# A new order of all 2328 operations of a gated attention/FFT kernel on one core

## The chip, the core and the metric

The kernel runs on one core of one Trainium2 chip. The metric is the device time of one execution in microseconds (us), and the time of a kernel is the median of several executions. One profiled execution is recorded beside them. In it every instruction has a start, a duration and an engine: TensorE (PE, with its weight loads PEld), VectorE (DVE), ScalarE (ACT), GpSimd (POOL) and SyncE (SP, which here only issues DMAs).

## What is computed

The input x has 2048 rows of 640 bf16 values. Two branches work on it, and a gate of its own for each row mixes them:

```python
g = _sigmoid((x * gate_w).sum(-1, keepdims=True))
a = _A_ref(x, A_wq, A_wk, A_wv, A_wo, A_beta)
b = _B_ref(x, B_w_r, B_w_i)
return g * a + (1 - g) * b
```

Branch A is attention with 32 heads of 20 dimensions over four segments of 512 rows, with a memory that is carried from segment to segment:

```python
for s in range(N):
    qs, ks, vs = ...
    p = _softmax(jnp.einsum('bhqd,bhkd->bhqk', qs, ks) * scale + mask, axis=-1)
    a_dot = jnp.einsum('bhqk,bhkd->bhqd', p, vs)
    pq = phi(qs)
    a_mem = einsum('bhld,bhde->bhle', pq, M) / (einsum('bhld,bhd->bhl', pq, z)[..., None] + 1e-06)
    outs.append(g * a_mem + (1.0 - g) * a_dot)      # this g is sigmoid(beta), one for each head
    pk = phi(ks)
    M = M + einsum('bhld,bhle->bhde', pk, vs)
    z = z + einsum('bhld->bhd', pk)
return o @ wo                                       # o: the four outs, 2048 x 640
```

Branch B is a filter in frequency space: a two-dimensional real FFT of x, a product with the complex weights `w_r + i w_i`, and the inverse FFT.

## The kernel before

**A recorded program.** `Kern.record()` records the kernel as 2328 operations. An operation is a closure that writes one or more instructions, with what it reads and writes, a cost for each engine that may carry it, and a latency. `mms` (L495) records a group of matmuls; its instructions show as L514 in the profile, those of the output projection, which are split into four narrow matmuls, as L512. `copy_alts` (L519) gives a copy out of PSUM to ScalarE or VectorE; `one`, `either` and `small` record elementwise work; `dma` (L543) records a DMA, a transposing one (L546) or a plain one (L548). Nearly all DMAs are issued by SP; the two operations in `EARLY`, the first halves of the loads of wq and wk, may also be issued by ScalarE.

**An order written out.** `ORDER` (L578 to L677) is a list of 2328 numbers. Entry v stands for operation v//2, carried by its alternative v%2 (0 is the first engine of its list, 1 the second). `Sched.schedule` hands the operations to the queues of the engines in this order. Each engine carries out its queue strictly in that order, and an instruction that waits for a semaphore holds up all that stand behind it on the same engine. With the costs of the operations, `schedule` replays the list on a modelled clock; what comes out of the model is not the order but two allocations: which of eight PSUM banks (four for the logits, `qk`, four for all else, `gen`) an operation gets, and which of 56 DMA semaphores. A bank or a semaphore that was used before brings a wait for its former users:

```python
for v in order:
    o = ops[v // 2]
    o.eng = list(o.alts)[v % 2]
    queue[o.eng].append(o)
...
_, b.pool, b.bank = place(b, level)
...
o.dyn.extend(users.get(q, ()))
```

**The stages.** In the first 26 us SP loads x transposed (`xT`, segment 0 in three pieces), the weights and eight tiles of plain x (`xsb`, `ld_x`), which VectorE and GpSimd fold for the FFT. PE first runs ten matmuls on a zeroed tile, then the projections of segment 0 (`projd` in the code; `psum<-xT,wq` and `psum<-xT,wk`) as `xT` and the weights arrive. From then on attention and FFT are interleaved. The main work of attention for segment s and head group is: the logits (`qk`, matmuls that read `qkp`, the padded q and k that come back by `pad` DMAs from a scratch in HBM, `qk_scr`), the exponential on ScalarE (`ex`, L1263), the mask on GpSimd (L1284) and the products with v (`pv`).

**The end of the kernel.** The memory part of segments 1 to 3 goes over HBM: `st_part` and `ld_den` bring the denominators together, `den_gate` makes their reciprocals, `st_r` stores them (`r_scr<-rc`), `ld_r` loads them in another layout (`r<-r_scr`), and `normal` multiplies by them. The unnormalised output is stored (`st_u`) and loaded again (`ld_u`) for the rows, the memory output is written to `o_scr` (`st_o`) and comes back transposed by `oT` (`mT<-o_scr`, L546). The rows are finished in tiles of 128, by `finish_tile(s,a)` (L1506) for segment s and tile a of its four; operations are named with this pair below. `oT(s,a)` brings the tile's memory output, `addmem(s,a)` (L1534, `oU<-oU,mT`) adds it to the attention output, `Fb(s,a)` (`psum<-G,fbg`) makes the FFT branch's rows with the gate in them, `oproj(s,a)` adds the product with wo in the same PSUM bank, `final(s,a)` (`ot<-psum`) copies the bank out, and `st_out(s,a)` stores the tile (`out_dram<-ot`). Segment 3 takes its o by transposes on PE (`oT3`) and wo in another layout, which `ld_wo2` loads (800 KB).

**Entries that are spoken of below.** 24 and 25 are `ld_wka`, the first half of wk, on SP and on ScalarE; 26, 28 and 30 are the three `xT` loads of segment 0; 36 is `ld_beta`; 46 is the `ld_x` of the first fold; 3392 is a `pad` of segment 3; 4028 is `ld_r(0)`; 4418 and 4452 are `oT(1,3)` and `oT(2,3)`; 4288 is `st_out(2,1)`; 4510 is `ld_wo2`.

Of the kernel before, what the change touches and what calls it, by code (L numbers as in the profile page):

```python
# [461 lines left out]
class Kern:  # L462
# [10 lines left out]
    def b(self, *key):  # L473
        v = self.bufs.get(key)
        if v is None:
            v = self.bufs[key] = Buf(str(key))
        return v
# [20 lines left out]
    def mms(self, items, r, w, prio, name="", extra=0.0, mode=0):  # L498
# [17 lines left out]
        op = self.Sc.op({"pe": (f, cost, 141.0)}, r=r, w=w, prio=prio, name=name, mode=mode)  # L516
# [25 lines left out]
    def dma(self, dst, src, nbytes, r, w, prio, tr=False, name="", after=(), queue="sp"):  # L542
        def f(e):  # L543
            d_, s_ = dst(), src()
            if tr:
                return e.dma_start_transpose(d_, s_)  # L546
            with self.nc.allow_non_contiguous_dma(reason="small strided loads"):
                return e.dma_start(d_, s_)  # L548
        cost, work, width = self.QUEUE[name] if name in self.QUEUE else self.QUEUE[name, nbytes]
        queues = ("sp", "act") if name in self.EARLY else (queue,)  # L550
        return self.Sc.op({e: (f, cost, 0.0) for e in queues}, r=r, w=w, prio=prio, nbytes=nbytes, name=name, after=after,
                          dma=True, xfer=work, hold=tr and nbytes > 500000, width=width)
# [27 lines left out]
        46, 0, 90, 26, 74, 23, 2, 4, 36, 24, 6, 8, 28, 10, 12, 72, 14, 16, 30, 18, 20, 178, 64, 34, 202, 66, 68, 44, 42, 70, 93, 214, 52, 190, 48, 94,  # L580
        204, 97, 216, 180, 192, 218, 104, 98, 182, 76, 206, 101, 194, 38, 208, 220, 196, 103, 198, 222, 201, 184, 224, 186, 210, 188, 296, 50, 212,
        256, 298, 362, 78, 300, 536, 32, 80, 274, 538, 258, 83, 302, 260, 262, 276, 130, 278, 264, 84, 54, 280, 106, 266, 282, 1904, 86, 304, 364,
        284, 88, 366, 108, 380, 306, 576, 132, 826, 268, 290, 828, 814, 110, 368, 578, 831, 816, 113, 382, 384, 386, 819, 370, 540, 388, 832, 270,
        834, 410, 412, 272, 836, 414, 416, 391, 418, 552, 372, 490, 420, 288, 492, 494, 114, 496, 498, 554, 118, 820, 822, 134, 336, 500, 240, 137,
        338, 242, 340, 120, 348, 58, 824, 342, 116, 350, 308, 122, 312, 544, 142, 226, 932, 546, 124, 344, 292, 244, 56, 228, 144, 246, 286, 248, 347,
        139, 352, 230, 294, 232, 126, 250, 354, 146, 234, 374, 1906, 149, 237, 1908, 356, 254, 1910, 359, 2094, 151, 238, 1912, 844, 1914, 252, 2124,
        140, 2126, 1916, 2128, 128, 2130, 360, 166, 2096, 40, 846, 2098, 154, 2132, 848, 2100, 2134, 1924, 326, 1926, 314, 2102, 168, 392, 1928, 2104,
        1930, 156, 892, 310, 1932, 152, 838, 1944, 1934, 170, 334, 1946, 158, 894, 840, 324, 316, 1948, 842, 808, 897, 161, 328, 810, 1950, 1952, 394,
        320, 813, 880, 886, 163, 882, 322, 1954, 888, 560, 332, 502, 884, 504, 396, 506, 330, 172, 508, 890, 448, 376, 510, 1936, 398, 450, 436, 512,
        438, 378, 402, 452, 514, 562, 440, 174, 442, 2162, 400, 1962, 2164, 176, 444, 2166, 516, 556, 454, 456, 2168, 446, 165, 2170, 458, 464, 460,  # L590
        466, 406, 1918, 468, 462, 470, 570, 472, 408, 2172, 910, 912, 542, 474, 898, 900, 318, 914, 602, 903, 2150, 548, 604, 2152, 2154, 2156, 2158,
        1920, 2178, 572, 404, 2160, 1966, 2180, 1958, 2182, 1922, 1968, 574, 904, 60, 2184, 2174, 2186, 906, 594, 2188, 1956, 564, 908, 1970, 2176,
        580, 934, 874, 596, 876, 1972, 879, 476, 566, 1974, 62, 478, 480, 550, 1977, 868, 870, 930, 422, 568, 482, 424, 873, 484, 426, 928, 916, 558,
        486, 428, 430, 488, 918, 2136, 432, 598, 2138, 920, 2140, 434, 2142, 856, 582, 858, 1960, 2144, 922, 519, 861, 924, 606, 584, 2146, 936, 1938,
        520, 2148, 926, 588, 523, 1020, 525, 608, 586, 652, 591, 2596, 802, 654, 862, 850, 804, 864, 852, 1940, 2216, 867, 2204, 2206, 2218, 2208,
        2220, 1942, 2210, 2222, 1980, 854, 2224, 2212, 656, 634, 2226, 2214, 1978, 778, 658, 2006, 2228, 636, 780, 2230, 2008, 1982, 2190, 2010, 782,
        2012, 526, 946, 2014, 786, 784, 2192, 948, 1964, 938, 940, 942, 2194, 788, 950, 2196, 945, 2198, 952, 600, 660, 2017, 2200, 790, 662, 2202,
        792, 2018, 976, 978, 1984, 794, 2020, 958, 798, 796, 1986, 960, 980, 954, 2233, 800, 1988, 982, 610, 956, 664, 2038, 612, 1990, 528, 2236,
        2234, 1992, 965, 530, 984, 986, 2040, 1995, 534, 2076, 988, 2078, 962, 2042, 1996, 2000, 1998, 2044, 991, 614, 618, 1016, 2080, 2024, 620,
        2002, 996, 1014, 2082, 2238, 638, 998, 2084, 972, 2004, 2022, 2046, 622, 668, 974, 992, 624, 2086, 2049, 2056, 626, 1018, 994, 1070, 1072,  # L600
        2058, 1074, 666, 2060, 1022, 1076, 642, 1002, 2050, 806, 1104, 1024, 1026, 670, 645, 1001, 2062, 532, 1028, 2270, 2064, 1031, 628, 2036, 2636,
        2252, 2240, 1106, 2272, 630, 2638, 2274, 2254, 640, 2066, 2276, 2106, 676, 616, 2640, 2256, 678, 592, 2258, 1010, 1004, 2243, 2026, 966, 968,
        2052, 2070, 2028, 1013, 632, 692, 971, 1006, 694, 680, 2244, 2642, 1009, 2644, 686, 1032, 2068, 1034, 682, 2246, 646, 1100, 2054, 2090, 1036,
        2030, 2088, 684, 2288, 649, 710, 2034, 2646, 672, 2290, 1039, 2566, 712, 674, 2292, 2598, 2294, 2600, 2306, 2072, 2602, 2110, 2604, 2308,
        2606, 2074, 2568, 2310, 700, 2092, 2108, 2312, 714, 2608, 726, 2112, 2786, 703, 716, 728, 2114, 1044, 2788, 2570, 688, 1062, 1064, 1046, 2790,
        696, 1066, 2792, 2794, 2650, 1069, 690, 1040, 2796, 650, 2574, 734, 1042, 1110, 698, 1078, 736, 1108, 1082, 730, 1080, 1112, 1114, 1118, 1102,
        1120, 732, 1122, 1116, 750, 1084, 1124, 2260, 2032, 738, 752, 2278, 1049, 2578, 2262, 2280, 2264, 2580, 2282, 704, 2266, 1051, 2284, 2268,
        2296, 2582, 744, 706, 1148, 1150, 2298, 718, 2586, 2648, 754, 2300, 1058, 720, 2302, 3288, 1152, 1089, 2616, 1061, 2618, 1126, 1155, 740,
        1130, 1052, 746, 1132, 1054, 2620, 2572, 1056, 2332, 1086, 1204, 1128, 748, 1206, 2334, 1208, 2622, 2624, 2250, 756, 1096, 1211, 1090, 1135,
        1192, 1092, 2627, 762, 2118, 1095, 2576, 2610, 2390, 1194, 1137, 1098, 1196, 765, 1198, 2392, 1200, 2314, 2120, 2698, 1203, 722, 2700, 2628,  # L610
        1138, 2316, 2702, 2318, 742, 1156, 2122, 1158, 2320, 1160, 1140, 724, 708, 1163, 2704, 2630, 2324, 2612, 2116, 1142, 1168, 2654, 2614, 2706,
        770, 2326, 1170, 1164, 758, 1166, 2842, 2844, 2846, 2848, 761, 2850, 2658, 2652, 2328, 2364, 2852, 766, 2676, 2330, 2366, 2709, 2678, 1280,
        2660, 2584, 2680, 2662, 2712, 2590, 1175, 2870, 2664, 1278, 2592, 2666, 2632, 2682, 2656, 2668, 2348, 1190, 2684, 2634, 2350, 2854, 2336,
        2710, 2856, 2858, 2860, 2862, 2672, 2286, 2896, 2687, 2898, 2864, 2358, 2340, 2866, 2872, 1274, 2352, 2868, 2342, 2874, 2876, 2360, 2882,
        2816, 768, 2884, 2818, 2362, 2878, 2820, 2688, 2886, 2880, 2888, 2822, 2890, 1188, 2692, 2824, 2690, 2900, 2344, 2826, 2902, 2904, 2670, 2382,
        2368, 2828, 2892, 2384, 2830, 2894, 2832, 2346, 2748, 2834, 2906, 2750, 1242, 2370, 1244, 1246, 2752, 2674, 2836, 2376, 2694, 1248, 2716,
        2838, 2696, 2448, 2714, 772, 2338, 2754, 2354, 2450, 2730, 2732, 2356, 2840, 2734, 2736, 2756, 1173, 2738, 2372, 2741, 2758, 2386, 2422, 2588,
        2378, 2375, 1144, 2760, 2394, 1176, 2742, 1147, 2768, 1186, 2770, 2424, 2718, 2772, 2322, 2774, 2802, 2776, 2744, 1178, 2764, 3290, 2779,
        2594, 1234, 3292, 1236, 774, 1238, 2798, 2762, 2746, 2406, 2782, 3328, 1276, 1241, 2408, 3294, 3296, 2766, 3298, 2720, 3330, 2780, 3301, 1182,
# [361 lines left out]
    def gate(self, s, t_end):  # L981

        self.Sc.group += 1
        b = self.b
        prio = t_end - 1.0
# [17 lines left out]
        bank = Bank(1, "gen")  # L1003
        items = []
# [602 lines left out]
```

## Time and profile before

| | us |
| --- | --- |
| median of three runs | 243.88 (243.15 to 245.06) |
| span of the profiled execution | 245.4 |
| PE busy | 228.8 (93%), 4347 matmul instructions |
| PEld busy (beside PE) | 140.8 (57%) |
| ScalarE busy | 199.9 (81%) |
| VectorE busy | 195.6 (80%) |
| GpSimd busy | 166.4 (68%) |

The profiled execution is 1.5 us longer than the median, and 0.3 us longer than the slowest of the three runs. Times of the profile are read against its own span.

PE is the engine that is busy almost throughout; it stands still for 245.4 - 228.8 = 16.6 us in all. Busy time of matmuls is modelled at their ends, so a busy PE need not be PE at its peak. The DMA engines moved 42.2 MB, 172 GB/s on average. The costliest group is the exponential (138.7 us of ScalarE), the mask is 122.1 us of GpSimd, and neither of them fills its engine.

### The profile page before, as it was taken

How to read it: one execution, taken by the hardware profiler on the slowest of the kernel's cores; microseconds unless marked ns; L12 is line 12 of the kernel's file. 1: busy time of each engine (PE TensorE's matmuls, PEld its weight loads, DVE VectorE, ACT ScalarE, POOL GpSimd, SP SyncE). 2: the span in 40 equal slices, each digit the busy share in tenths (PEclk: the TensorE clock that was granted, in tenths of full speed). 3: DMA queues.
4: the chain of work that ended last, by engine and by line, in shares of the span. 5: the costliest groups of instructions: out<-in, count | busy, mean ns of one | idle time of the engine just before them, and what ended most of it. 6: DMA issues, size and time to landing. Idle time of an engine off the chain costs nothing.

```text
span 245.4 us, 10243 instructions
## 1 busy us (share of the span) xinstructions
PE 228.8 (93%) x4347; PEld 140.8 (57%) x4361; DVE 195.6 (80%) x481; ACT 199.9 (81%) x241; POOL 166.4 (68%) x297
## 2 busy tenths in 40 slices
PE   7899999999999999999899999899999997699994
PEld 2574567765455665545556555465454565366794
DVE  0479998889999987989999898989889867435563
ACT  2289698988999999999899889999999976388740
POOL 8513268557969846768947998859898694359730
PEclk9999999999999999999999999999999999589999
DMA  7999959975799875575698661375758997812123
GB/s 168 278 365 208 239 160 178 318 140 164 210 200 174 168 226 143 125 199 135 202 233 234 185 186 53 99 210 146 222 151 194 230 140 96 127 36 85 57 84 108
DMA packets 58928, 42.17 MB, mean 172 GB/s; under 512 B 30020, under 2 KB 55172, under 8 KB 58884
## 3 DMA queue, kind: packets, MB, share of 16 engines
q1 hardware_dynamic: 57844, 40.96, 69.2%
q8 instruction: 34, 0.56, 1.0%
q10 hardware_dynamic: 1040, 0.57, 0.8%
q14 instruction: 10, 0.08, 0.1%
HBM read 23.32 MB, written 12.30 MB: 145 GB/s over the span
## 4 chain that ended last, share of the span: by engine, by line
PE 54%; DVE 18%; ACT 12%; DMA 10%; issue 3%; SPq 1%; DVEq 0%
PE psum L514 48%; ACT ex L1263 9%; PE psum L512 6%; DMA pkn<-phk 4%; DMA r_scr<-rc 3%; DMA xT<-in_A_x_dram 2%; DVE xsb L906 2%; DVE Pt L1439 2%; DVE xf L901 1%; DVE phk L1085 1%; ACT et L1072 1%; DVE oU L1526 1%; DVE G L1485 1%; DVE ub L525 1%; DVE va L1115 1%
## 5 line engine op out<-in xcount | busy, mean ns | idle before, releaser
L1263 ACT ACTIVATE ex<-psum 128x2048 bf16<-128x2048 f32 (+4 forms) x92 | 138.7, 1507 | 16.3 <-PE psum L514 14.3
L1284 POOL TENSOR_SCALAR_AFFINE_SELECT ex<-ex 128x256 bf16<-128x256 bf16 (+2 forms) x224 | 122.1, 567 | 42.0 <-ACT ex L1263 38.4
L514 PE MATMUL psum<-qkp 20*64 20x64 bf16 (+5 forms) x1280 | 32.7, 271 | 4.8 <-issue 2.3
L514 PE MATMUL psum<-xT,wk 128*128 128x256 bf16 (+1 forms) x280 | 34.0, 273 | 0.9 <-DMA wk<-in_A_wk_dram 0.6
L514 PE MATMUL psum<-wv,xT 128*32 128x321 bf16 (+3 forms) x400 | 30.0, 301 | 0.6 <-DVE va L1115 0.3
L514 PE MATMUL psum<-xT,wq 128*128 128x512 bf16 (+1 forms) x121 | 27.0, 380 | 1.3 <-DMA xT<-in_A_x_dram 0.7
L1439 DVE TENSOR_TENSOR Pt<-psum,Wt 128x642 bf16<-128x642 f32 x32 | 25.5, 820 | 2.3 <-PE psum L514 1.9
L514 PEld LDWEIGHTS psum<-qkp 20*64 20x64 bf16 x1280 | 13.4, 103 | 19.5 <-ACT ex L1263 13.2
L514 PEld LDWEIGHTS psum<-xT,wk 128*128 128x128 bf16 (+1 forms) x280 | 19.9, 97 | 7.0 <-DMA wk<-in_A_wk_dram 1.1
L512 PE MATMUL psum<-wo,oU 128*32 128x320 bf16 x480 | 23.4, 313 | 0.5 <-DVE oU L1534 0.5
L906 POOL TENSOR_TENSOR xsb<-xf 128x320 bf16<-128x320 bf16 (+2 forms) x12 | 9.2, 763 | 17.1 <-DVE xsb L906 13.2
L525 DVE CAST ot<-psum 128x320 bf16<-128x320 f32 x21 | 10.1, 491 | 12.9 <-PE psum L512 10.5
L514 PEld LDWEIGHTS psum<-wv,xT 128*32 128x32 bf16 (+1 forms) x400 | 14.3, 96 | 8.3 <-issue 2.4
L514 PE MATMUL psum<-big,Ac 128*128 128x160 bf16 (+2 forms) x96 | 18.1, 258 | 0.7 <-DVE Pt L1439 0.3
L1115 DVE TENSOR_TENSOR va<-psum,ebx 128x320 bf16<-128x320 f32 x32 | 15.2, 483 | 4.2 <-ACT gate L1113 2.1
L514 PE MATMUL psum<-big,Cp 128*128 128x321 bf16 (+1 forms) x96 | 18.0, 302 | 0.2 <-DVE G L1485 0.2
L514 PE MATMUL psum<-ex,va 128*32 128x64 bf16 (+3 forms) x576 | 17.4, 256 | 0.7 <-DVE dn L1152 0.3
L1485 DVE TENSOR_TENSOR G<-eo,psum 128x320 bf16<-128x320 f32 x32 | 14.7, 482 | 3.9 <-PE psum L514 2.8
L512 PEld LDWEIGHTS psum<-wo,oU 128*32 128x32 bf16 x480 | 12.4, 100 | 8.8 <-issue 4.2
L514 PE MATMUL psum<-tt,Yt 128*128 128x256 bf16 (+1 forms) x96 | 16.5, 275 | 0.3
L514 PEld LDWEIGHTS psum<-ex,va 128*32 128x32 bf16 x576 | 11.1, 96 | 9.7 <-POOL ex L1284 3.4
L1072 ACT ACTIVATE et<-qu 128x512 bf16<-128x512 bf16 x25 | 15.6, 630 | 0.2
(99 smaller groups left out, 391.9 us busy)
## 6 DMA issues: line engine op xcount, KB each, us to landing
qkp<-qk_scr SPq DMA_DIRECT2D x28, 160.0 KB
tt<-tab_tt SPq DMA_DIRECT2D x8, 512.0 KB, 4.3
qk_scr<-qu SPq DMA_DIRECT2D x12, 256.0 KB, 3.1
u_scr<-ub SPq DMA_DIRECT2D x12, 256.0 KB, 3.9
xsb<-in_A_x_dram SPq DMA_DIRECT2D x8, 320.0 KB, 6.8
oU<-u_scr SPq DMA_DIRECT2D x15, 128.0 KB, 2.9
out_dram<-ot SPq DMA_DIRECT2D x12, 160.0 KB
Wt<-in_B_w_r_dram SPq DMA_DIRECT2D x16, 80.2 KB, 2.6
```

What stands on the lines that cost most here:

```text
L512: h = e.matmul(dst, wt, r_, start=st, stop=sp_, **{**kw, "tile_position": (0, q), "skip_group_check": True})
L514: h = e.matmul(o_, l_, r_, start=st, stop=sp_, **kw)
L525: alts["dve"] = (lambda e: e.tensor_copy(dst(), src()), 67 + 1.04 * n, 68.0)
L901: self.either(lambda e, r=r, op=op: e.tensor_tensor(xf.ap(r * 642, [321, 2], [1, 320]), xs.ap(o, [D, 2], [1, 320]), xs.ap(o + 320, [D, 2], ...
L906: self.either(lambda e, dst=dst, src=src, d0=d0, n=n, op=op: e.tensor_tensor(xs.ap(o + dst, [D, 2], [1, n]), xf.ap(src + d0, [321, 2], [1, ...
L1072: self.one("act", lambda e: e.activation(et.ap(0, [1, L]), qsl(), ACT.Exp), L, [qb], [b("et", pi_)], late, name="phi_exp")
L1085: fmin = lambda e: e.tensor_tensor(dst(), dst(), et.ap(0, [1, L]), ALU.min)
L1115: self.one("dve", lambda e: e.tensor_tensor(va.ap(i * H * VW + h0 * VW, [VW, nh], [1, DH]), self.ps(bank, 0, [DH, nh], [1, DH]), self.ebx. ...
L1263: self.one("act", lambda e, d=d, q=q: e.activation(self.ex.ap(*d), self.ps(bank, *q), ACT.Exp, scale=SC), n, [bank], [self.exb(s, 2 * pr + ...
L1284: self.one("pool", lambda e: e.affine_select(self.ex.ap(e0 + d0, [1280, 4], [1, n], np_=np_), self.ex.ap(e0 + s0, [1280, 4], [1, n], np_=np_),
L1439: self.one("dve", lambda e, ri=ri, Pt=Pt, Wt=Wt, wo_=wo_, bank=bank: e.tensor_tensor(Pt.ap(ri * 322, [644, 2], [1, KD]), self.ps(bank, 0, ...
L1485: self.one("dve", lambda e, q=q, n2=n2, bank=bank, eo=eo: e.tensor_tensor(self.G.ap(n2 * D + 639 * q, [1 - 2 * q, 320]), eo.ap(q, [1, 320] ...
```

## The change

Every entry of `ORDER` is written anew. The multiset of operations is the same; 131 of the 2328 change their engine (folds, copies out of PSUM, parts of `final`, gate arithmetic, and `ld_wka` from SP to ScalarE). SP goes from 232 to 231 operations, ScalarE from 249 to 246, VectorE from 481 to 485, GpSimd and PE keep their numbers. The median operation moves by three places in its engine's queue. No operation computes anything else, and none is added or left out.

Four edits beside it change costs that only the replay reads: the logits' matmuls cost 22 ns more and have a latency of 216 ns instead of 141, every DMA costs 60 ns more on its queue (110 for `st_qk`, `st_u` and `ld_u`), the first exponential of `phi` has a fixed part of 94 ns instead of 65, and the transposing matmul of the gate is taken to have the array pattern 2 instead of 0. They write no instruction differently; with the new order they change which bank and which DMA semaphore an operation gets.

```diff
@@ -513,7 +513,7 @@
-        op = self.Sc.op({"pe": (f, cost, 141.0)}, r=r, w=w, prio=prio, name=name, mode=mode)
+        op = self.Sc.op({"pe": (f, cost + 22.0 * (name == "qk"), 216.0 if name == "qk" else 141.0)}, r=r, w=w, prio=prio, name=name, mode=mode)
...
@@ -547,6 +547,7 @@
...
+        cost += 110.0 if name in ("st_qk", "st_u", "ld_u") else 60.0
...
@@ -577,103 +578,103 @@
...
-        46, 0, 90, 26, 74, 23, 2, 4, 36, 24, 6, 8, 28, 10, 12, 72, 14, 16, 30, 18, 20, 178, 64, 34, 202, 66, 68, 44, 42, 70, 93, 214, 52, 190, 48, 94,
...
-        3094, 3536, 1550, 3142, 3080, 1552, 1520, 1555, 1488, 1522, 3286, 1556, 1525, 3096, 1558, 3118, 1584, 3082, 1490, 1560, 3434, 3084, 3392,
...
-        3612, 4030, 1620, 1644, 3170, 1654, 1623, 1646, 4028, 3654, 1656, 1648, 3160, 3184, 4042, 3584, 3656, 1658, 1650, 3162, 3670, 3250, 3658,
...
-        1768, 3676, 4510, 1770, 1866, 1772, 4216, 4026, 4050, 3596, 4064, 4052, 4054, 4218, 3466, 3680, 1774, 3752, 1832, 4158, 3682, 1834, 3700,
...
-        4358, 4360, 4362, 3864, 4186, 4258, 4364, 4366, 4368, 4189, 3866, 4418, 3920, 4370, 1884, 3858, 4490, 3922, 4276, 4322, 4260, 4372, 4262,
-        3868, 4374, 4452, 4376, 4378, 4380, 4264, 4278, 4382, 4280, 4492, 4266, 3924, 4385, 3834, 4282, 3934, 3836, 4268, 4324, 4270, 4326, 3833,
-        4162, 4273, 4328, 4284, 4330, 4164, 4287, 4166, 3870, 4168, 4332, 4170, 4288, 4334, 3816, 3842, 3838, 4336, 4402, 3844, 4404, 3872, 4406,
...
+        0, 23, 26, 74, 2, 25, 4, 28, 6, 8, 10, 12, 72, 14, 30, 16, 18, 20, 46, 190, 34, 104, 90, 202, 76, 44, 36, 52, 48, 204, 206, 178, 192, 214,
+        194, 216, 180, 218, 38, 208, 196, 182, 210, 198, 213, 184, 200, 220, 186, 92, 222, 188, 94, 224, 536, 96, 98, 42, 380, 538, 256, 101, 32,
...
+        3416, 1524, 3572, 3172, 3436, 3574, 3442, 3152, 3562, 3576, 3174, 1612, 3444, 3154, 1615, 3446, 3622, 3578, 4028, 1606, 3581, 1608, 3449,
+        3583, 1574, 3196, 3430, 1610, 3624, 1577, 3156, 3606, 3176, 3392, 3626, 3158, 1652, 3628, 1654, 1634, 1636, 2562, 1638, 3178, 3608, 3614,
...
+        4287, 4270, 3924, 3834, 4272, 4493, 4324, 3868, 4326, 3836, 4288, 4328, 4162, 3870, 4380, 4164, 4330, 4418, 4382, 4166, 3934, 4332, 4385,
+        4338, 4340, 4334, 3926, 4402, 4168, 4337, 3842, 4452, 3816, 4170, 3874, 4342, 3844, 4172, 4344, 3838, 4404, 4175, 4388, 4346, 4390, 4392,
+        4190, 4290, 4406, 3846, 3848, 4394, 4348, 4396, 4510, 4398, 4408, 3840, 4292, 4350, 3878, 4352, 4304, 4420, 4306, 3880, 4294, 3876, 4401,
...
@@ -1004,7 +1005,7 @@
...
-        self.mms(items, [b("hi", s), b("lo", s), b("fcat"), bank], [], prio + 4.0, name="gateT")
+        self.mms(items, [b("hi", s), b("lo", s), b("fcat"), bank], [], prio + 4.0, name="gateT", mode=2)
...
@@ -1070,7 +1071,7 @@
...
-                     late, name="phi_exp")
+                     late, fix=94, name="phi_exp")
...
```

In the new list the start has 25 (`ld_wka` on ScalarE) and all three `xT` loads ahead of 46 (`ld_x`) and 36 (`ld_beta`); 3392 stands behind 4028; 4418 and 4452 stand directly behind 4288 on SP, while before they stood directly ahead of it; and 4510, which before stood ahead of the store and reload of the reciprocals of segment 2, is the second of SP's operations behind 4452.

## The prediction

> **What bounds the kernel now.** I read the shares of the chain that ended last first, then the slices of the span, then the two ends of the kernel operation by operation, because that is where PE stands still.
>
> ```profile
> PE   7899999999999999999899999899999997699994
> PEclk9999999999999999999999999999999999589999
> ...
> PE 54%; DVE 18%; ACT 12%; DMA 10%; issue 3%; SPq 1%; DVEq 0%
> ```
>
> Each digit of the first two lines is a fortieth of the span, 6.1 us. PE is full but for the first slices, the last, and slices 34 and 35, where its granted clock falls to 0.5 as well. PE idles 16.6 us in all; of these 3.0 lie before 8 us, 3.7 between 200 and 211.4, and 3.1 behind the last matmul. What is left, 6.8 us, is spread over many short gaps. So a new order of the same operations has three places to win or lose in: the start, the stretch from 204 us on, and the fit of the long middle, where PE is never free for long.
>
> The start, as SP's queue of DMA issues and PE's timeline show it (start, duration, operation, and in brackets the idle time before it and who ended it):
>
> ```profile
> 0.79 0.40 SPq L548 DMA_DIRECT2D xsb<-in_A_x_dram  x1
> 1.25 1.22 SPq L546 DMA_TRANSPOSE xT<-in_A_x_dram  x1
> 2.52 0.57 SPq L548 DMA_DIRECT2D beta<-in_A_beta_dram  x1
> 3.14 0.42 SPq L548 DMA_DIRECT2D wk<-in_A_wk_dram  x1
> 3.61 2.95 SPq L546 DMA_TRANSPOSE xT<-in_A_x_dram  x2
> ```
>
> ```profile
> 7.81 0.40 PE L514 MATMUL psum<-xT,wq 128*32 128x512 bf16 x4 [0.42 <-DMA xT<-in_A_x_dram]
> ```
>
> PE waits .33, .57 and .42 us at its first three projections, and the last piece of xT, issued by 6.56 us, releases it at 7.81.
>
> The end: PE's timeline, the stretches around its stall (us, busy time and count of PE, PEld, DVE, ACT, POOL, granted clock, DMA share, GB/s), the DMA answers for 204.1 to 208.7 us, and the transposes that run there.
>
> ```profile
> 208.75 0.32 PE L514 MATMUL psum<-qkp 20*64 20x64 bf16 x23
> 211.41 0.21 PE L514 MATMUL psum<-qkp 20*64 20x64 bf16 x1 [2.35 <-issue]
> ```
>
> ```profile
> 209.40:211.40 2.00, 0.00 (x0) 0.00 (x0) 0.55 (x2) 0.00 (x0) 0.41 (x1) 0.50 0.90 103
> 211.40:216.20 4.80, 4.79 (x69) 2.43 (x72) 1.39 (x4) 2.74 (x4) 1.50 (x3) 0.50 0.75 117
> 216.20:223.00 6.80, 6.80 (x205) 4.45 (x197) 2.60 (x6) 5.56 (x6) 5.34 (x10) 1.00 0.20 49
> ```
>
> ```profile
> q1 hardware_dynamic: 804, 0.46, 87.3%
> ...
> mT<-o_scr SPq DMA_TRANSPOSE x2, 7.2
> ```
>
> The stall of 2.35 us falls between matmul 23 and 24 of one operation; the 24th waits for no semaphore, hence "issue". I read it as PE short of instructions. The profile has a queue of 34 instruction packets of 16 KB, that is one for every 256 instructions of PE by the counts of this trace. Mostly one starts 0.3 to 1.5 us after PE crosses into a new block; here PE crossed at 204.12, no packet ran in the window above, where two mT transposes were landing, and it ran at 208.76, 4.64 us late. PE then ran again 1.5 us after it had come. The clock stayed at 0.5 until 216.2: 4.8 us of busy PE at half rate are about 2.4 us lost. Stall and clock together cost 4.75 us.
>
> **The change part by part.** All prices are against the profiled 245.4 us. The median of the runs is 1.52 below it, and I subtract that at the end.
>
> *Start.* Ahead of the second xT load SP loses the issues of ld_x (.40), beta (.57) and the first half of wk (.42): 1.40 us. ScalarE issues that half of wk second in its queue and has nothing else to do then. SP's xT issues would be done at 0.79 + 1.22 + 1.35 + 1.56 = 4.92 instead of 6.56. The gain lies between nothing (transfers, not issues, set the landing) and 1.64. I take 1.40, because 320 KB less (the x tile) also stand ahead of it: 1120 KB instead of 1440 before the projections have all their data. The first fold's x lands some 4 us later, the others 1.4 earlier. Folds run on VectorE, which the chain passes through between 17.9 and 36.2 us; VectorE's work ahead of the last fold is 26.05 us before and 25.87 after, so the fold can wait without making that stage longer. If that fails, the stage swallows the gain.
>
> *Middle.* PE's slots move by 0.64 us at the median, 160 of 1073 operations by over 2 us. Of the moved engine work, VectorE gets 4.0 us more (224.2 to 228.2, summed from measured durations by operation), ScalarE 1.8 less, GpSimd 2.2 less. None of these is full, so 0; ends -1 and +1, from the 6.8 us of scattered gaps. The planner's edited costs write no instruction. PE changes its array pattern 231 times instead of 229; PEld's gaps put down to issue average 0.24 us (17.5 us over 72), so +0.2, bounds 0 and 0.5.
>
> Three moves are hidden. The pad of segment 3 goes behind ld_r(0), ready at 166.8 us; its logits come at 170.7, about 4 us of cover against 3 us to landing; if it isn't enough, up to 1.5. ld_wo2 goes from 187.8 to about 222; by the 291 to 395 GB/s of the slices around its transfer its 800 KB need 2 to 3 us beyond the 3 of a small load, and its first reader runs at 235.4: 7 us to spare. Ahead of the store of the reciprocals (194.85, landed 201.76, reload to 204.13, PE waiting .54 at 208.09) that leaves 800 KB and some u loads less; gain 0 to 0.5, inside the ends of the next step.
>
> *The stall.* PE's blocks are counted in instructions, and their number before the stage is the same but for a few. The boundary again falls into pv(3,3), the next into qk(3,2,3). Whether the fetch comes late depends on the transposes that run then. In the new order oT(2,1) stands ahead of st_out(1,1), and the wo2 transfer is away, so they come earlier by up to one store's wait. I work out a stall of 0 to 2.0 us and take 1.0, a gain of 1.35, rounded to 1.3. The clock loss of 2.4 us is kept, because in the trace three gaps of .29 to .54 us stand ahead of the stall, and PE would be late at all of them. Ends: nothing gained, and 4.75.
>
> By the Trainium skill ("TensorE: Matmul & The Clock Gate", "Part 1: The HAM clock gate") the clock halves after one idle window of about 3.4 us. Here a 2.35 us gap sufficed, beside shorter ones. By the page a stall of 1.0 us would leave the clock whole, and the sum would be 2.4 us lower; the row decides and I keep the loss.
>
> *The two late transposes.* This is what speaks against the change.
>
> ```profile
> L546 SPq DMA_TRANSPOSE mT<-o_scr x8: 1200/1246/2332, 167.8 to 215.0; - x8
> ...
> DMA to landing us min/median/max: 3.8/5.5/7.2
> ```
>
> ```profile
> 211.58 4.64 SPq L546 DMA_TRANSPOSE mT<-o_scr  x2
> 219.90 9.42 SPq L548 DMA_DIRECT2D out_dram<-ot  x5
> ```
>
> Before, oT(1,3) and oT(2,3) are issued at 211.6 and 215.0. Now they are queued behind st_out(2,1), which waits for final(2,1). Before, that store goes at 219.90; in the new order its last matmul stands 1.2 us earlier on PE, so it goes at 218.7 and the two at about 219.3 and 220.5. By the 3.8 to 7.2 us to landing, the second arrives between 224.3 and 227.7. addmem(2,3) takes .48, its first oproj comes at 228.2: cover 0 to 3.4 us. I price it at 0. If the two don't overlap on the DMA queue, the second lands at 230.3 to 233.7, and PE is late by 2.6 to 6.0. VectorE is in order too: behind the waiting addmem(1,3) stand final(0,3) and the pv quotients.
>
> *Sum:* 245.4 - 1.4 - 1.3 + 0.2 = 242.9; less 1.52 is 241.4.
>
> **The rivals.**
>
> *A. No change, 243.9.* The start's gain ends in the VectorE stage (18% of the chain), and the stall comes where it was, because the plan moves PE by only 0.64 us. For it: PE is 93% busy and nothing is removed. Against it: PE's waits at the start are for DMAs that SP issues late.
>
> *B. Slower, 247.0.* mT(2,3) comes after 227.7. From there on each us later is a us on the path. Its price is 4.3, the middle of 2.6 to 6.0, and where transposes crowd each other the stall stays too: 241.4 + 1.3 + 4.3 = 247.0. For it: 7.2 us to landing is measured for such a pair in the window above, and in the row of 211.58 the second of the two went out only 3.4 us behind the first. Against it: the DMA share is 0.20 there between 216 and 223 us, and single transposes land in 3.8 to 5.5.
>
> *C. Much faster, 237.9.* The fetch comes in time, no stall, full clock: 245.4 - 1.4 - 4.75 + 0.2 = 239.45, less 1.52.
>
> *D. The planner's order doesn't carry over to the chip.* The durations it holds are of single instructions, and what PE lost here, the fetch, is none of them. That is the case for A over the forecast, and I put no extra time on it.
>
> **How the numbers follow.** Forecast .38, C .20, A .20, B .22. The forecast alone runs from 239.9 (start 1.64, stall gone but clock kept, patterns 0) to 243.3 (half the start's gain, a stall of 2.0 us, patterns +0.5). The range from 237.5 to 247.0 takes in C and A, and B up to its mid price; outside lie half of B and the best of C. This kernel's runs can't tell changes of under about 1% (2.44 us) from none, so the limits are 241.44 and 246.32. Half of the forecast lies below 241.44 and half above it: faster .19 + .20, about .40; same .19 + .17 of A, .36; slower is B and a little of A, .24.
>
> **What would show it.** Start: the last xT wait of PE ends by 6.5 us instead of 7.81, and the fold stage ends earlier by as much. Stall: "issue" at PE around 209 us is under 2 us, and the time at clock 0.5 is as long as before; under C both are gone. Transposes: no PE idle on mT or on addmem at 228 us; B would show it there, with mT landing after 227.7. I am wrong if PE's idle elsewhere grows by more than 1 us, which no row here would have told.

## The result and the profile after

| | before | after |
| --- | --- | --- |
| median | 244.47 us (4 runs, 243.15 to 246.54) | 253.43 us (4 runs, 252.32 to 256.06) |
| ratio | | 1.0427 (95%: 1.034 to 1.051) |
| span of the profiled execution | 245.4 us | 250.3 us |

The new order is 4.3% slower: 253.43 us, where the forecast was 241.4 and its range ended at 247.0. The two profiles that stand here differ by only 4.9 us, less than the medians, and this has a reason that the prediction needed: each later run lists its time and its span, and the time is 1.7 to 2.5 us above the span, 2.0 in the changed kernel's profiled execution (252.32 and 250.3). The profiled execution of the kernel before, with a span of 245.4, took some 247.4, then, 3.5 us more than the 243.88 that the prediction set beside it. A second profile of the same kernel (run e17, below) has a span of 241.0 and a granted clock of 1.0 up to the last matmul. I compare with that one from here on. Of 70 executions of the kernel before, four took over 246.5 us, and the ratios here and below leave out executions that took over 1.5% longer than the fastest of their kernel, while the medians don't.

The slices of the span and the shares of the chain, after:

```profile
PE   7999999999898999997899998999989899898994
...
PEclk9999999999999999999999999999999999799799
...
PE 23%; DVE 8%; DMA 7%; ACT 7%; issue 2%; SPq 1%; POOL 0%; DVEq 0%
```

And of e17, the kernel before:

```profile
PE   7899999899999999999999999899999999899994
...
PEclk9999999999999999999999999999999999999999
...
PE 51%; DVE 18%; DMA 11%; ACT 11%; SPq 4%; issue 3%; ACTq 0%; DVEq 0%
```

Two things show. In the new order PE drops below 9 tenths again and again, from slice 11 on. And the clock falls to half in two stretches near the end, of 3.41 us each (from 213.76 and from 230.83); each costs about 1.7 us, half its length. The mean clock tells how many such stretches an execution has: of the four of the changed kernel two have 0.986, that is two stretches, and two have 0.98, three. The shares of the chain tell no difference: those of the changed kernel add up to 48%, because its chain is followed back only to 125 us, and of that part PE has 23 in 48, much as it has 51 in 98 in e17.

The waits of the weight loads, which stand ahead of the matmuls, by what ended them (us, times, longest), first e17, then after:

```profile
PEld psum L514 <- issue: 16.0, 67, 0.4
PEld psum L514 <- ACT ex L1263: 14.0, 46, 0.6
PEld psum L514 <- POOL ex L1284: 4.0, 12, 0.5
PEld psum L514 <- DVE Pt L1439: 3.7, 15, 0.6
```

```profile
PEld psum L514 <- issue: 23.7, 93, 1.6
PEld psum L514 <- ACT ex L1264: 8.8, 29, 0.7
...
PEld psum L514 <- DVE va L1116: 2.7, 6, 1.1
PEld psum L514 <- DVE mem L1158: 2.3, 5, 0.7
```

Summed over all rows of this view, the weight loads (PEld) idle 64.8 us in e17 and 70.9 us after, 6.1 more: +5.2 for VectorE (19.7 to 24.9), +7.8 with no releaser that the profile shows ("issue", 73 to 100 times), -4.0 for ScalarE, -2.3 for DMAs, -0.6 for GpSimd. The last matmul ends at 237.80 in e17 and at 247.14 after. Of these 9.3 us the half clock is 3.4, and 6.1 are waits: 9.5 together. PE's own idle time, span less busy time, grows less, from 14.3 us (241.0 - 226.7) to 18.0 (250.3 - 232.3). But the trace of e17 has records of 4347 matmuls only, as the first profile, of the 4361 that PE runs, and the time of the other 14 counts as idle there; the weight loads are complete in both traces. Either way this is the sign of being wrong that the prediction named, PE's idle growing by more than 1 us elsewhere.

Where they lie I read by giving each of PE's operations its slot, from its first weight load to that of the next operation, and comparing it with the slot of the same operation in e17. By 10 us the new order is 1.5 us ahead. It loses 3.3 from 10 to 120, 1.0 from 120 to 190, 2.4 from 190 to 200, and 4.1 behind that, the half clock among it. No single wait of a matmul is above 1.3 us.

A single wait can belong to one execution, though. Behind the start, the longest of PE in the changed kernel's profile is one for a pad:

```profile
81.81 0.42 PE L514 MATMUL psum<-qkp 20*64 20x320 bf16 x16 [1.26 <-DMA qkp<-qk_scr]
```

None of the seven other profiles below that have the new order there, with this pad at its place (e1, e3, e5, e10, e12, e13, e14), has this wait. In the same way e17 waits 1.01 us for a pad at 46.75, and of seven other profiles with the old order there (the first one, e2, e4, e6, e8, e11, e18) only e11 waits for it, 0.54 us. So the loss of a stretch is known to about 1 us: from 10 to 120 us it is 3.3 beside e17, and 3.9 to 4.7 beside the first profile, e2, e4, e8 and e18.

The start answers to what was shown of before: xT's three pieces go first on SP, and PE takes up the projections at 5.98 and never again waits for xT.

```profile
0.78 4.24 SPq L546 DMA_TRANSPOSE xT<-in_A_x_dram  x3
5.06 0.58 SPq L548 DMA_DIRECT2D xsb<-in_A_x_dram  x1
```

```profile
5.98 0.40 PE L514 MATMUL psum<-xT,wk 128*32 128x256 bf16 x8 [0.27 <-DMA xT<-in_A_x_dram]
...
11.12 0.43 PE L514 MATMUL psum<-qkp 20*64 20x512 bf16 x12 [0.48 <-ACT qkp L523]
```

The tail: SP's issues (start, duration), the landing of the transposes, and PE's stall.

```profile
201.43 1.09 SPq L548 DMA_DIRECT2D r_scr<-rc  x1
...
206.16 0.51 SPq L548 DMA_DIRECT2D r<-r_scr  x1
206.72 0.60 SPq L548 DMA_DIRECT2D oU<-u_scr  x1
...
221.49 3.09 SPq L546 DMA_TRANSPOSE mT<-o_scr  x2
```

```profile
DMA to landing us min/median/max: 3.0/3.1/4.2
```

```profile
213.51 0.32 PE L514 MATMUL psum<-G,fbg 128*32 128x320 bf16 x4 [1.16 <-DVE on L1326]
```

The two late transposes, from which the slower rival came, went out at 221.49 and some 223.3, landed after 3 to 4 us, and PE waited for neither. Another thing was late: the store of the reciprocals went at 201.43 (194.76 in e17) and one of the u loads of segment 2 stood behind their reload, at 206.72. All five u loads were out by 194.6 in e17. Here it is on VectorE:

```profile
211.75 0.42 DVE L1527 TENSOR_TENSOR oU<-oU,r 128x512 bf16<-128x512 bf16 x1 [0.50 <-DMA oU<-u_scr]
212.28 0.49 DVE L1535 TENSOR_TENSOR oU<-oU,mT 128x640 bf16<-128x640 bf16 x1
212.69 0.25 DVE L1324 RECIPROCAL rs<-rs 128x16 f32<-128x16 f32 x1
212.97 0.49 DVE L1326 TENSOR_TENSOR on<-psum,rs 128x320 bf16<-128x320 f32 x1
```

The quotient (`on`, L1326) that PE waits for needs no u at all; it stands behind `normal` on VectorE's queue, and `normal` waits for the load. PE's matmul doesn't read the quotient either: by the replay, that `Fb` gets the PSUM bank out of which the quotient reads the products with v.

### The profile page after: what moved, and what is told of

Read it like the earlier page. It is cut to its first block, busy times and chain, and to the rows that moved or that the text cites. A ratio compares the mean times of both kernels' runs of the same rounds, so it can differ in the third digit from the quotient of the medians.

```text
span 250.3 us, 10261 instructions
## 1 busy us (share of the span) xinstructions
PE 232.3 (93%) x4361; PEld 141.4 (56%) x4361; DVE 203.5 (81%) x485; ACT 198.4 (79%) x237; POOL 166.4 (66%) x297
## 5 line engine op out<-in xcount | busy, mean ns | idle before, releaser
L514 PE MATMUL psum<-xT,wk 128*128 128x256 bf16 (+1 forms) x280 | 33.1, 273 | 0.8 <-DVE Pt L1440 0.4
L514 PE MATMUL psum<-xT,wq 128*128 128x512 bf16 (+1 forms) x135 | 31.3, 380 | 0.0
L1440 DVE TENSOR_TENSOR Pt<-psum,Wt 128x642 bf16<-128x642 f32 x32 | 25.4, 820 | 1.9 <-POOL ex L1285 1.1
L512 PE MATMUL psum<-wo,oU 128*32 128x320 bf16 x480 | 24.5, 322 | 0.5 <-POOL oU L1527 0.4
L907 POOL TENSOR_TENSOR xsb<-xf 128x320 bf16<-128x320 bf16 (+2 forms) x10 | 8.3, 838 | 17.0 <-DVE xf L902 8.4
L514 PE MATMUL psum<-big,Cp 128*128 128x321 bf16 (+1 forms) x96 | 18.6, 303 | 0.8 <-DVE eo L525 0.4
L514 PE MATMUL psum<-big,Ac 128*128 128x161 bf16 (+2 forms) x96 | 18.2, 258 | 0.9 <-DVE mem L1158 0.3
L514 PE MATMUL psum<-ex,va 128*32 128x64 bf16 (+3 forms) x576 | 17.6, 256 | 1.2 <-DVE dn L1153 0.7
L525 DVE CAST ot<-psum 128x320 bf16<-128x320 f32 x19 | 9.2, 487 | 10.7 <-PE psum L512 8.6
L514 PE MATMUL psum<-tt,Yt 128*128 128x256 bf16 (+1 forms) x96 | 15.9, 275 | 1.3 <-DVE Yt L1445 0.8
```

The source lines that it names most:

```text
L512: h = e.matmul(dst, wt, r_, start=st, stop=sp_, **{**kw, "tile_position": (0, q), "skip_group_check": True})
L514: h = e.matmul(o_, l_, r_, start=st, stop=sp_, **kw)
L525: alts["dve"] = (lambda e: e.tensor_copy(dst(), src()), 67 + 1.04 * n, 68.0)
L907: self.either(lambda e, dst=dst, src=src, d0=d0, n=n, op=op: e.tensor_tensor(xs.ap(o + dst, [D, 2], [1, n]), xf.ap(src + d0, [321, 2], [1, ...
L1440: self.one("dve", lambda e, ri=ri, Pt=Pt, Wt=Wt, wo_=wo_, bank=bank: e.tensor_tensor(Pt.ap(ri * 322, [644, 2], [1, KD]), self.ps(bank, 0, ...
```

## The experiments

Each ratio is to the kernel before, timed on the same chip. Numbers in the diffs are entries of `ORDER`; only their place in the queue of the engine that is named matters.

| run | what | median us (before) | ratio (95%) |
| --- | --- | --- | --- |
| e1 | new order, old costs | 253.19 (242.21) | 1.046 (1.043 to 1.049) |
| e2 | old order, new costs | 242.84 (242.21) | 1.004 (1.001 to 1.007) |
| e3 | new until 120 us | 245.50 (242.21) | 1.012 (1.006 to 1.017) |
| e4 | old until 120 us, then new | 250.93 (242.21) | 1.035 (1.027 to 1.042) |
| e5 | new, u loads early | 254.35 (243.03) | 1.038 (1.031 to 1.045) |
| e6 | old, xT first | 244.64 (243.03) | 1.009 (1.004 to 1.014) |
| e7 | new until 40 us | 243.35 (243.03) | 1.002 (0.999 to 1.005) |
| e8 | old, u loads late | 244.55 (243.03) | 1.007 (1.004 to 1.010) |
| e10 | new, 14 copies back on ScalarE | 255.03 (242.80) | 1.051 (1.047 to 1.055) |
| e11 | old, the 14 copies on VectorE | 247.51 (242.80) | 1.020 (1.016 to 1.024) |
| e12 | new until 190 us | 254.27 (242.80) | 1.047 (1.041 to 1.053) |
| e13 | e5 and e10 together | 253.58 (242.80) | 1.042 (1.036 to 1.048) |
| e14 | new, eight VectorE operations ahead | 250.95 (242.68) | 1.031 (1.025 to 1.038) |
| e15 | new, one pad earlier | 252.00 (242.68) | 1.037 (1.033 to 1.042) |
| e16 | e14, e15 and e5's edit | 251.57 (242.68) | 1.037 (1.030 to 1.045) |
| e17 | before again | two runs: 243.00 (profiled), 249.33 | |
| e18 | old, two W_adds at new places | 243.22 (243.18) | 1.001 (0.998 to 1.004) |

Where median and ratio say different things (e3, e5, e13, e14, e15), the ratio is to be read.

**The costs or the order: e1 and e2.** The changed costs could matter only through banks and semaphores.

```diff
 e1: after.py with
-cost + 22.0 * (name == "qk"), 216.0 if name == "qk" else 141.0
+cost, 141.0
-cost += 110.0 if name in ("st_qk", "st_u", "ld_u") else 60.0
 (and the two costs of gateT and phi_exp); e2: before.py with these edits the other way
```

> The new order replayed with the old costs: the queues of all engines are those of the changed kernel, only the banks and DMA semaphores that the replay gives are others. Theory M (the order itself loses in many small waits of PE): as the changed kernel, 252 to 255 us. Theory C (the edited costs give banks or semaphores whose waits lose the time): back to 243 to 246. Theory T (the two late transposes of the tail): 252 to 255, as M.

> The old order replayed with the new costs. Theory M: 243 to 245, no change. Theory C: 250 or more. Theory T: 243 to 245.

The order alone gives the whole loss (e1), the costs alone 0.4%. Theory C is out.

**Which half: e3, e4 and e12.** Up to a time T the operations that start before T in one trace stand in that kernel's order and on its engines, the rest in the other's.

```diff
+ORDER = [v for v in first if v // 2 in head] + [v for v in second if v // 2 not in head]
```

> All operations that start before 120 us in the changed kernel's trace stand in the new order and on the new engines, the others in the old order; old costs. Theory M, by the sum of PE's slots up to 120 us (2.5 us longer than the same operations' slots before): 246 to 247.5. Theory T: at or below the kernel before, 242 to 244.5, since the tail is the old one. Theory C: 243 to 245.

> The complement: the old order up to 120 us of the trace of before, the new one behind it, with the new costs. Theory M: the rest of the loss, 248 to 252. Theory T: all of the loss and the start's gain missing, 253 to 256. Theory C: 250 or more.

> All that starts before 190 us in the changed kernel's trace in the new order, the rest in the old. Theory M: PE's slots are 3.6 us longer by 190 us, and the old tail adds nothing: 246 to 247. Theory W (more than a third of the loss comes from the tail: waits there and half clock): as well 246 to 247, and the granted clock is 0.993 or above, against 0.98 to 0.986 in the changed kernel. If the old tail is no better behind a late start: 250 to 253.

Both halves are slower, and 1.2% and 3.5% add up to 4.7%, where e1 has 4.6%. So it isn't one place, and not the tail alone. In the traces most stretches of 10 us that keep their order keep their slots to 0.04 us, so that the edited part can be read; single ones differ by up to 1.1 us between two executions of the same kernel (the first profile and e17, from 40 to 50 us). e12 came out 7 to 8 us above its expectation, and it proves little: at its joint SP waits 3.2 us for a pad (issued at 194.4) with ld_den and the u loads behind it, a wait that neither kernel has. A joined order is a fair test only where the joint is clean, as in e3.

**The start: e6 and e7.**

```diff
 SP in e6
-46, 26, 36, 24, 28, 30, 34
+26, 28, 30, 46, 36, 34
 ACT
-23
+23, 25
```

> The kernel before with only its start changed: the three xT loads first on SP, the first half of wk on ScalarE. The prediction's step for the start, alone: -1.4 us, 240.8 beside 242.2. Rival A (the stage on VectorE up to 36 us swallows it): 241.9 to 242.5.

> All that starts before 40 us in the new order, the rest in the old. In the profile of the kernel that has the new order up to 120 us the start gains 2.3 us by 10 us and has given back all but 0.3 to 0.4 by 50. If these slots tell it, 241.5 to 242.5; if the start's gain is kept, 240 to 241.

The prediction's -1.4 isn't there. In e6 xT comes early, and the next load takes its place; PE's timeline of e6:

```profile
5.78 0.61 PE L514 MATMUL psum<-xT,wq 128*32 128x512 bf16 x8 [0.83 <-DMA xT<-in_A_x_dram]
...
12.05 1.25 PE L514 MATMUL psum<-xT,wk 128*128 128x256 bf16 x10 [1.75 <-DMA wk<-in_A_wk_dram]
```

PE stands 1.75 us for the second half of wk, which hadn't gained anything. With the new order of all engines up to 40 us (e7) the lead at 10 us is 1.5 us, and by 50 e7 is within 0.3 us of e17. e6 is even slower by 0.9%; in its profile a half clock of 3.41 us at 208.81 is part of that, and its six runs have mean clocks of 0.993 or less.

**SP's order in the tail: e5 and e8.** The same move in both directions. The reload that the second expectation calls ld_r(0) is the one of segment 2 (entry 4136).

```diff
 SP in e5
-4150, 3464, 4078, 3466, 4138, 3256, 3470, 4354, 4154, 4136, 4146
+4150, 4138, 4154, 4146, 3464, 3256, 4078, 3466, 3470, 4354, 4136
 SP in e8
-4150, 4154, 4146, 4142, 4138, 3256, 4078, 3468, 4354, 4136
+4150, 4142, 4078, 3468, 4138, 3256, 4354, 4154, 4136, 4146
```

> The changed kernel with four of SP's operations put back where they stood before: three loads of u for segment 2 go in a row with the other two, and the store of the reciprocals goes ahead of st_out(0,0). Theory S (SP's order in the tail makes normal(2,0) late, PE idles 1.16 us at 212.35 and then runs 3.41 us at half clock): the gap and the half clock go, 1.2 + 1.7 = 2.9 us or a little more, 249.5 to 251 us. Theory M (only many small waits of the whole order): no change, 252.5 to 254.

> The kernel before with the same four operations moved the other way, to the places that they have in the new order: three u loads of segment 2 behind st_out(0,0), oT(2,2) and ld_r(0), and the store of the reciprocals behind st_out(0,0). Theory S: addmem(2,0) comes 2 to 4 us later and PE stalls as in the changed kernel, 244 to 246. Theory M: 242 to 243.

In the old order it costs what theory S said, at the place it said. PE's timeline of e8, and its stretches (busy and count of PE, PEld, DVE, ACT, POOL, granted clock, DMA share, GB/s):

```profile
206.91 0.32 PE L514 MATMUL psum<-G,fbg 128*32 128x320 bf16 x4 [1.07 <-DVE on L1306]
```

```profile
204.00:207.50 3.50, 2.29 (x71) 1.55 (x67) 3.23 (x9) 2.24 (x3) 1.70 (x2) 1.00 1.29 99
207.50:211.00 3.50, 3.10 (x68) 1.68 (x72) 2.30 (x7) 1.63 (x3) 1.52 (x4) 0.52 0.48 123
```

An idle of 1.07 us, ended by the same quotient as in the changed kernel, and the clock is half in the next window. Measured: +0.7% (0.4 to 1.0), 1.7 us, as much as one such window costs. In the new order, undoing it took the 1.16 us stall at 212 away. Of five other profiles with this part of the new order, four have that wait for the quotient (e4 1.55 us, e1 1.27, e10 0.57, e15 0.46) and one doesn't (e14). A gain in time isn't shown: 1.038 beside 1.043, with intervals that overlap, and e5's four runs took 250.95, 252.61, 256.09 and 256.68 us. The half clock in its profile had moved to 201.02.

**VectorE's load: e10, e11, e13.** VectorE's durations, summed by operation, rose from 225.3 us in e17 to 232.7.

```diff
 entries of e10 (e11 the other way)
-285, 1955, 953, 2647, 2669, 2759, 3339, 3319, 1335, 3373, 3411, 1469, 1585, 3449
+284, 1954, 952, 2646, 2668, 2758, 3338, 3318, 1334, 3372, 3410, 1468, 1584, 3448
```

> The changed kernel with 14 copies out of PSUM (ten of the projections, four of stage D) back on ScalarE, where they were before; VectorE sheds some 8.9 us (10 x 0.69 + 4 x 0.49), about as much as it had gained. Theory D (VectorE is late because of what was moved to it; PE's waits on VectorE are 6.7 us longer than with the old order): 2 to 4 us faster than the changed kernel, 249.5 to 251.5. Theory M (positions, not load): within 1 us of it or slower, 252.5 to 256, since the copies now queue behind exponentials.

> The reverse dose: the kernel before with the same 14 copies moved to VectorE at their old places. Theory D: 2 to 4 us slower than before, 244.5 to 246.5. Theory M: less than 1 us.

> Both repairs of the new order at once: the 14 copies on ScalarE, and the u loads and the store of the reciprocals at their old places on SP. If D and S add: 247.5 to 250. Theory M: 252 to 254.

e11 goes theory D's way and beyond it: +2.0%, 4.7 us where it had 2 to 4. e10 says no: relieving VectorE in the new order made it no faster than the changed kernel (1.051 beside 1.043, with intervals that overlap), where theory D had 2 to 4 us of gain. The weight loads' idle rose to 74.4 us, less than after behind VectorE (23.2 instead of 24.9), more behind ScalarE (16.9 instead of 14.2) and GpSimd (7.5 instead of 4.3). Both repairs together (e13, 1.042) gain nothing that shows. So VectorE's load alone isn't the loss of the new order. It may be that in either order the engine of an operation and its place are fitted to each other; that would fit e10 and e11, but isn't shown.

**Single repairs of the new order: e14, e15, e16.**

```diff
 VectorE in e14, each X directly ahead of Y (operations)
+1129 ahead of 1026, 1461 of 610, 611 of 626, 734 of 719
+736 ahead of 1674, 796 of 1714, 910 of 2048, 2038 of 2050
 SP in e15
-2114, 1100, 1190, 2036
+2036, 2114, 1100, 1190
```

> The changed kernel with eight VectorE operations moved ahead in VectorE's queue, each of which ended one of PE's largest waits and had stood behind others with its inputs ready (W_add 611 for 2.72 us, ev_v 1461 for 0.98, final 2038 for 1.91, ev_Db 910 for 1.67, mem_mul 1129 for 1.95, W_mul 736 for 1.10, ev_D 734 and 796 for 0.30 and 0.47). PE's waits there sum to 4.8 us. Theory Q (the order of VectorE's queue makes these waits, and PE can't make them up): 3 to 4.5 us faster than the changed kernel, 249 to 250.5. Theory M' (what was ahead is then late in its turn): within 1.5 us of 253.4.

> The changed kernel with one pad of segment 1 moved on SP ahead of a load of W that waits 1.90 us; PE stands 1.26 us at 80.55 for this pad. Theory Q: 1 to 1.3 us faster, 252 to 252.5, and the gap at 80.55 is gone from PE's timeline. Theory M': the gap goes and comes back elsewhere, 253 to 254.

> The repairs of the two runs before and the early u loads of the tail in one kernel. Theory Q: 4.8 + 1.3 + 1 to 3 us in all, 245 to 248. Theory M': 251 to 253.5.

e14 wins some 1.2 to 1.5 points back: 1.031 beside 1.043, with intervals that overlap, and beside 1.046 for the same order in e1, with intervals that don't. That is about what theory Q had said, but not for its reason. The weight loads' idle is 71.2 us, not less than the 70.9 of the changed kernel. The slots of the same operations are 2.2 us shorter from 50 to 120 us, 1.5 from 190 to 200 and 2.0 behind that, and longer by 0.4 from 10 to 50 and by 2.8 from 120 to 190. What is gone in its profile is the half clock, 3.4 us in the changed kernel's: it is 1.0 up to the last matmul. Its four runs have mean clocks between 0.987 and 1.0, those of the changed kernel 0.98 to 0.986. e15's profile, of an execution of 256.58 us, the longest of its five, has no gap at 80.55. But that gap is in no profile of the new order save the changed kernel's own, so there was nothing to repair, and 1.037 beside 1.043, with intervals that overlap, shows no gain. Putting all together (e16, 1.037) adds nothing. So local waits can be removed, and PE meets others instead. No version beat the kernel before.

**One misplaced pair, and an ordinary profile: e18 and e17.**

```diff
 VectorE in e18 (operations)
-626, 1402, 611, 610, 1461
+626, 610, 1402, 1461, 611
```

> The kernel before with two of VectorE's W_adds (610 and 611) where the new order has them: 610 ahead of phi_min(1402), 611 behind ev_v(1461). Theory Q, with GpSimd in the way: 611 takes 0.7 to 1.5 us instead of 0.32, PE waits for it near 115 us, and the kernel is 0.8 to 1.5 us slower, 243.3 to 244.2. Theory M': under 0.4 us.

> The kernel before, unchanged, for one more profile. If the stall of 2.35 us at 209 and the half clock belonged to one execution: a span near 240.5, a granted clock of 1.0, and no idle of PE over 1.3 us from 200 us on. If they belong to the kernel: they are there again and the span is 244 or more.

e18 changed nothing, and it is inconclusive. W_add 611 took 0.44 us there and not 1.5. It ended just behind the mask of 0.46 us that ran on GpSimd as it started, though the next mask followed that one without a gap. The dose wasn't given. e17 confirms that the stall of 2.35 us belonged to that execution: span 241.0, clock 1.0, and no idle of PE above 0.54 us from 200 us to the last matmul. The place recurs, though: at the same matmul, the 24th of its operation, PE waits 0.36 us in e6 and 0.69 in e7, also with no releaser. The prediction had read the stall as a late packet of instructions, and the DMA records fit that: the packet came at 208.76 there, and at 205.13 in e17, 204.45 in e6 and 204.74 in e7. What made it late no run shows.

## Why the prediction was wrong

**The step that failed is the middle, priced at 0 with ends of -1 and +1.** It was bounded by the 6.8 us of scattered idle time that the kernel before has (7.2, since 2.6 and not 3.0 us lie before 8 us), as if a new order could only shift that. A new order can add to it. Measured, the waits ahead of PE grew by 6.1 us, spread over the whole kernel; e3 and e4 show that both halves carry a part. I had weighed the named moves one by one, and none of them was found to carry the loss. The same step took 4.0 us more work on VectorE as free; its durations grew by 7.4, and e10 shows that taking 14 copies off it again doesn't help. No row of the trace of before could have given the sum, and a median shift of 0.64 us of PE's slots said nothing of it either: the operations that PE waits for are small parts of queues of four other engines.

**The stall wasn't there to be won.** I credited 1.3 us for a shorter stall, and took the profiled execution to be 1.52 us from the median. It was some 3.5 us from it, since time and span are two scales. The stall and its clock, 4.75 us by the prediction's own count, are about the 4.4 us by which the span of 245.4 exceeds e17's. So the median doesn't have the stall; with the offset of about 2 us, which the later runs list, one subtraction tells that.

**The clock** loss was put down as kept, the same before and after. That was wrong in both kernels: the old order mostly runs at full clock, and the new one has two or three stretches of 3.41 us at half, 3.4 us of the 9 in the profile. Nor was it the 2.35 us gap that halved the clock in the first profile, as the prediction reads it: the clock fell at 209.42, when that gap (209.06 to 211.41) was 0.36 us old.

**The start** was right in its direction and place (PE 1.5 us ahead at 10 us) and wrong in what lasts: waits for the second half of wk (1.75 us in e6), for ScalarE's copy into `qkp` (0.48 at 11.12 after) and in the stage behind take it back. Rival A had said that the gain would end in that stage. **The late transposes** went out 2.2 and 2.8 us later than worked out and were hidden, as priced. **ld_wo2** was hidden too: no wait of PE is for it. **The reciprocals** I took for a possible gain of 0 to 0.5, because 800 KB were out of their way; the u loads that left their place ahead of the store came back behind it, and the same move costs 1.7 us in the old order (e8). I had counted bytes ahead of the store and hadn't asked who waits for the loads that went. **Rival B** has the right sign and the wrong mechanism, and at 247.0 not half of the loss.

What stays open: why the new order's waits are many. It is shown that they come from the order, in both halves, that shedding VectorE doesn't cure them and that removing eight of the largest lets others grow. Which rule the old order keeps and the new one breaks wasn't found. The weight loads' idle without a releaser (17.6 to 25.4 us, of which 1.6 are the pad wait at 80.55) is the largest part of the growth, mostly ahead of the logits (13 to 24 times) and of the products with v of segments 0 to 2 (6 to 12); by the code the array pattern changes 231 times instead of 229, so it isn't the number of changes. That operations on VectorE take longer, beside GpSimd perhaps (3.0 us in all, below), may be a part; e18, which was to test it, didn't bring it about.

## What to carry to other kernels

Before a profile is used as the base, put its own time beside the runs, on one scale; a stall in an execution 3.5 us above the median need not be the kernel's. The same goes for a single wait that is to be repaired: the 1.26 us at 80.55 stands in one profile of eight. Where one engine is 93% busy and its order is rewritten throughout, the named moves are not the price: here small waits in all parts added up to more than any of them, and the new list had to be run to know it. Joining two orders at a time where the joint is clean locates such a loss in two runs, and moving one thing in both directions, as with the u loads, tells whether it costs by itself, even where taking it back gains nothing that shows.

## What the runs showed of the hardware

The half clock comes in stretches of 3.41 us or two or three of them. Their grid doesn't start with the kernel: full clock begins between 4.0 and 7.3 us in these profiles. From 196 us on, an idle of 0.99 us or more of PE inside one window of 3.41 us was mostly enough for the next to be at half, in 14 windows of 16: 0.99 in e6 (208.81), 1.18 in e8 (207.48), 1.16 after (213.76), 1.64 in e4 (214.15). The sum of the idle doesn't decide alone. The same 0.99 us (two waits, of 0.41 and 0.58) was followed by half clock in e5 and e13 and not in the changed kernel (from 196.69 on) and e10; three times 0.51 to 0.56 was enough (e1 at 213.03, after at 230.83, e18 at 206.93), and 0.94 in e3, from 206.81 on, was not. Earlier, 1.75 us of idle from 112.28 on (e5) and 1.16 from 80.64 on (after) cost nothing; the one early drop in all these traces is in e12, at 116.55, behind 1.74 us. The Trainium skill ("TensorE: Matmul & The Clock Gate", "Part 1: The HAM clock gate") says that the window is free-running and 3413 ns long, which agrees; that the half rate follows an idle window, which these numbers contradict: no window here was idle throughout.

W_add, a sum of two SBUF tensors on VectorE, takes 0.32 us (median of four in the changed kernel) when GpSimd is free and 0.60 (median of twelve, 0.31 to 1.54) when GpSimd is at work as it starts. The longest, in the changed kernel (VectorE, then GpSimd):

```profile
114.19 1.54 DVE L1445 TENSOR_TENSOR Yt<-Pt 128x321 bf16<-128x321 bf16 x1
```

```profile
113.91 0.66 POOL L1285 TENSOR_SCALAR_AFFINE_SELECT ex<-ex 64x512 bf16<-64x512 bf16 x1
114.55 0.39 POOL L992 TENSOR_TENSOR ebg<-gate,ebx 128x128 f32<-128x128 f32 x1
114.90 0.66 POOL L1285 TENSOR_SCALAR_AFFINE_SELECT ex<-ex 128x512 bf16<-128x512 bf16 x1
```

It ends at 115.73, just behind the last of three GpSimd operations that follow each other without a gap, and PE waits 0.76 us for it. The Trainium skill ("Trainium Architecture — The Big Picture", "What this means for kernel authors") calls the port that the two share an exclusive lock; this row, in which W_add ends only behind the GpSimd work, agrees. Why it waits for three operations here (1.54 us in e1, e3, e5 and e15 as well) and in e18 for the first alone, no run shows. For an order this means that what an operation costs on VectorE depends on what stands on GpSimd at that moment. Of the 7.4 us that VectorE's durations grew, 3.0 are the same operations taking longer; how much of that is GpSimd's doing wasn't measured.
